# Attention's output and gathered expert tiles turned by transposing transfers, in a fused attention, feed-forward and expert kernel

## The chip, the cores and the metric

The program runs on one core of a Trainium2 chip. The metric is the device time of one execution in microseconds: before the change 768.54 us, the median of 3 runs (767.34 to 770.0). The profiled execution is a run of its own: 772.55 us, of which 770.8 us lie between its first and its last instruction (the span).

## The reference

```
B, H, S, D = 4, 8, 768, 48
# attention: a decayed running state, one 48x48 matrix for each of 32 heads
for t in range(S):
    state = alpha[:, :, t, :, None] * state + einsum('bhd,bhe->bhde', k[:, :, t], v[:, :, t])
    y[:, :, t] = einsum('bhd,bhde->bhe', q[:, :, t], state)
x = y.transpose(0, 2, 1, 3).reshape(3072, 384)
# first feed-forward: w_in 384x2048, w_out 2048x384
h = x @ w_in
x = maximum(0.01 * h, h) @ w_out
# eight experts, each token goes to the one with the largest logit; w1 384x1024, w2 1024x384
logits = x @ w_gate
e = argmax(logits); gate = softmax(logits)[e]
out[token] = gate * (maximum(x[token] @ w1[e], 0) @ w2[e])
```

All inputs and the output are float32. The kernel holds most matrix operands as pairs of float16, a high and a low part, and multiplies high by high, high by low and low by high. So each product of the feed-forward and of the experts is three matmuls.

## The kernel before

**Units.** The 3072 tokens are cut into 8 units of 384. For a unit, attention works on three chunks of 128 tokens, and then the first feed-forward takes the unit as a whole. For one chunk, `chunk` makes scores on TensorE (L710), masks them on VectorE (L715, L717), multiplies them with the values (L741 in units 2 to 7, L747 in units 0 and 1) and adds what the state gives (L754). This leaves the 128x384 result `yp` in PSUM with tokens on the partitions. VectorE takes the largest absolute value (L763), ScalarE writes the scaled result as float32 to `xh` (L767), TensorE turns it in three 128x128 pieces (L777; L775 in units 0 and 1), and ScalarE and VectorE write the high and low parts of the turned result to `xT` (L781, L789). The feed-forward's first product, "hidden" below, reads `xT` (L825, 144 matmuls a unit), its second product reads the activated `gh` (L834, 144 matmuls a unit).

**Routing.** After a unit's second product `route` picks each token's expert and scatters its row (float16 high and low part, gate, token number) with three indirect transfers on GpSimd's queue (L967) to a table `x2_rows` in HBM, ordered by expert. `gather` fetches 128 rows of one expert into a tile `acc` with an indirect transfer (L1198), for which `place_of` copies the tile's row numbers on VectorE (L1195). `turn` turns a gathered tile on TensorE with six float16 transposes (L1212) and copies the result on ScalarE to `XT` (L1214).

**Experts.** There are 26 tiles. 14 of them (`NA`) are full with the rows of units 0 to 6 alone and are gathered before the last unit's scatters; 12 are gathered after these, and 4 of these 12 are split between two experts. The experts' inner width of 1024 is worked off in 4 phases of 256, and each phase passes over all 26 tiles: 104 steps of 18 matmuls (L1334, "hidden") and 6 wider ones (L1363). A step also copies a slice of W1 chosen by a register (`stage`, L1251, VectorE), takes the relu in two parts (L1342 on ScalarE, L1346 on VectorE), and adds into `acc` (L1374 to L1381). For split tiles a second slice comes by a transfer from SBUF to SBUF (`so`, L1261). While one phase runs, the next phase's weights are loaded in 16 pieces of 384 KB on SyncE's queue (L1093) through three buffers and split into high and low parts (in phase 0 on ScalarE L1129 and VectorE L1505, later also on GpSimd).

**What sets the order.** Every engine works off its instructions in the order in which they are written. Up to the end of the feed-forward that order comes from a planner, `Loom`: each piece of work is a generator that yields operations `O` with an engine letter (P TensorE, V VectorE, A ScalarE, G GpSimd, D SyncE's transfers), an assumed duration, and rings of buffers that it takes and frees; the planner keeps a clock for each engine. From the first expert step on the order is written out in `experts`, one pass of its loop for each step; `AHEAD1` says how many steps after a tile's gather its turn is written.

## Time and profile before

| | |
|---|---|
| median of 3 runs | 768.54 us |
| profiled execution: time, span | 772.55 us, 770.8 us |
| TensorE busy | 745.1 us, 97% of the span |
| VectorE, ScalarE, GpSimd busy | 607.2, 483.0, 378.7 us |
| transfers | 102.67 MB, 133 GB/s on the mean |
| granted TensorE clock, mean | 0.995 of full |

In a row of the profile stand the start and the duration of an instruction or a group, the engine, the line of the kernel, output and input by name, and in brackets how long the engine sat idle before it and what released it. Matmuls overlap one another, so the times from start to start tell what one costs TensorE, and not the durations. Transfers show the instruction that issues them; when their bytes have landed is seen at whoever waits for them.

### The profile page before, as it was taken

The numbers are of one execution on the slowest core, as the hardware profiler recorded it, in microseconds if no ns is written. First come the engines' busy times: TensorE is split into PE (matmuls) and PEld (weight loads), VectorE is DVE, ScalarE is ACT, GpSimd is POOL, SyncE is SP. The second block draws the span as 40 slices with busy tenths as digits, with TensorE's granted clock in tenths as the row PEclk, the third lists the DMA queues.
The fourth block names the chain that finished last, engine by engine and source line by source line (L and its number), as shares of the span: only waits on it lengthen the run. The fifth ranks groups of instructions, "written<-read, shape, count | busy, mean of one in ns | idle before, by whom it ended". The sixth has DMA issues, their size and how long they took to land.

```text
span 770.8 us, 21013 instructions
## 1 busy us (share of the span) xinstructions
PE 745.1 (97%) x7927; PEld 509.1 (66%) x7927; DVE 607.2 (79%) x1435; ACT 483.0 (63%) x1083; POOL 378.7 (49%) x406
## 2 busy tenths in 40 slices
PE   9999999998999999999999999899999999999994
PEld 4656675665666666656766665557777777777773
DVE  8999986599799879759855547756878899888673
ACT  4877576789866856845864645824676566667530
POOL 9135024451742763571581270553442588786543
PEclk9999999999999999999999999999999999999998
DMA  9914331153436234223001225224287555653341
GB/s 365 372 55 123 125 125 59 61 168 124 158 100 222 73 102 167 84 83 123 3 21 32 63 70 162 78 83 130 93 280 244 169 170 164 192 185 122 130 178 69
DMA packets 53131, 102.67 MB, mean 133 GB/s; under 512 B 4893, under 2 KB 37715, under 8 KB 53024
## 3 DMA queue, kind: packets, MB, share of 16 engines
q1 hardware_dynamic: 39360, 74.03, 29.9%
q0 software_dynamic: 4960, 14.62, 5.5%
q10 hardware_dynamic: 8704, 12.58, 4.8%
q8 instruction: 67, 1.10, 0.6%
q14 instruction: 40, 0.33, 0.1%
HBM read 79.17 MB, written 9.86 MB: 115 GB/s over the span
## 4 chain that ended last, share of the span: by engine, by line
PE 80%; DVE 11%; DMA 3%; issue 2%; ACT 2%; POOL 1%; ACTq 0%; DVEq 0%; POOLq 0%
PE m L834 22%; PE m L825 21%; PE a L1334 12%; PE m L1363 11%; PE a L710 3%; PE m L390 2%; PE a L754 2%; DMA wr<-in_moe_w 2%; PE a L669 1%; PE a L741 1%; PE a L637 1%; DVE st L1251 1%; DVE w L417 1%; DVE w L419 1%; PE a L486 1%
## 5 line engine op out<-in xcount | busy, mean ns | idle before, releaser
L834 PE MATMUL m<-woh,gh 128*128 128x392 f16 x1152 | 201.8, 329 | 0.0
L825 PE MATMUL m<-xT,wih 128*128 128x384 f16 x1152 | 193.8, 326 | 2.5 <-DVE gf L804 2.5
L809 POOL TENSOR_TENSOR gh<-gf,gh 128x384 f16<-128x384 f32 x128 | 119.0, 940 | 132.6 <-ACT gh L807 129.1
L825 PEld LDWEIGHTS <-wih 128*128 128x128 f16 x1152 | 111.8, 98 | 76.0 <-issue 4.7
L834 PEld LDWEIGHTS <-gh 128*128 128x128 f16 x1152 | 110.3, 98 | 73.4 <-issue 1.4
L1363 PE MATMUL m<-W,hs 128*128 (+1 forms) x624 | 119.1, 326 | 3.2 <-issue 1.8
L1334 PE MATMUL a<-XT,st 128*128 128x128 f16 (+1 forms) x1872 | 117.3, 215 | 3.0 <-DVE st L1251 1.6
L1334 PEld LDWEIGHTS <-st 128*128 128x128 f16 x1872 | 105.9, 98 | 21.0 <-issue 4.7
L804 DVE SCALAR_TENSOR_TENSOR gf<-m,gf 128x384 f32<-128x384 f32 x128 | 70.1, 554 | 55.6 <-ACT gf L802 55.4
L1251 DVE COPY st<-W 128x1536 f16 x104 | 82.7, 795 | 27.4 <-PE a L1334 16.2
L802 ACT ACTIVATE gf<-m 128x384 f32<-128x384 f32 x128 | 62.3, 489 | 42.9 <-PE m L825 39.1
L1342 ACT ACTIVATE hs<-a 128x256 f16<-128x256 f32 x104 | 39.7, 383 | 73.6 <-PE a L1334 52.8
L1363 PEld LDWEIGHTS <-hs 128*128 128x128 f16 (+1 forms) x720 | 57.6, 101 | 32.4 <-issue 3.0
L807 ACT CAST gh<-gf 128x384 f16<-128x384 f32 x128 | 64.4, 507 | 7.4 <-DVE gf L804 7.2
L1133 POOL TENSOR_TENSOR W<-wr,W 128x768 f16<-128x768 f32 x32 | 57.2, 1790 | 7.7 <-ACT W L1132 7.7
L1198 POOL DMA_INDIRECT acc<-x_rows,offj x26 | 30.3, 1164 | 37.3 <-DVE offj L1195 28.4
L1346 DVE SCALAR_TENSOR_TENSOR hs<-a,hs 128x256 f16<-128x256 f32 x104 | 43.2, 415 | 6.1 <-ACT hs L1342 5.4
L1106 POOL TENSOR_SCALAR wr<-wr 128x768 f32<-128x768 f32 x32 | 30.5, 952 | 27.7 <-DMA wr<-in_moe_w 14.9
L351 ACT ACTIVATE scrap<-W 128x768 bf16<-128x768 f16 x48 | 40.2, 838 | 5.9 <-ACT hs L1342 5.5
L1384 POOL DMA_INDIRECT out<-acc x26 | 26.5, 1019 | 31.7 <-DVE acc L1381 20.9
L967 POOL DMA_INDIRECT x_rows<-xg,pi x24 | 25.7, 1071 | 24.7 <-issue 6.4
L728 POOL TENSOR_TENSOR sh<-sm,sh 128x512 f16<-128x512 f32 x17 | 23.4, 1387 | 27.1 <-ACT sh L723 27.1
(279 smaller groups left out, 1238.6 us busy)
## 6 DMA issues: line engine op xcount, KB each, us to landing
wr<-in_moe_w SPq DMA_DIRECT2D x64, 384.0 KB
so<-W ACTq DMA_DIRECT2D x32, 384.0 KB
al<-in_aT SPq DMA_DIRECT2D x16, 390.0 KB
raw_in<-in_moe_w_in SPq DMA_DIRECT2D x12, 512.0 KB
kn__125<-in_kT SPq DMA_DIRECT2D x8, 768.0 KB
qn__126<-in_qT SPq DMA_DIRECT2D x8, 768.0 KB
raw<-in_moe_w_out SPq DMA_DIRECT2D x16, 384.0 KB
ck<-in_moe_w_in SPq DMA_DIRECT2D x24, 256.0 KB
```

The source lines that it names most:

```text
L351: A.activation(scrap, src, AF.Square, scale=scale, accum_out=g_sq[:, i : i + 1])
L802: A.activation(gf, ph[:, 0:UT], AF.Copy, scale=0.01 * CG)
L804: V.scalar_tensor_tensor(gf, ph[:, 0:UT], CG, gf, ALU.mult, ALU.max)
L807: A.copy(gh[:, 0], gf)
L809: E_[e].tensor_tensor(out=gh[:, 1], in0=gf, in1=gh[:, 0], op=ALU.subtract)
L825: T.matmul(ph[:, 0:UT], wih[:, a, kk, f * P : (f + 1) * P], xT[:, b, kk, :], start=(n == 0), stop=(n == 8),)
L834: T.matmul(po[:, 0:ROW], g[f][:, a, c * P : (c + 1) * P], woh_[0][:, b, f, :], start=(n == 0), stop=(n == 3 * NF - 1),)
L1133: G.tensor_tensor(out=lo, in0=raw, in1=hi, op=ALU.subtract)
L1251: V.tensor_copy(out=sth[i % 2].rearrange("p a k f -> p a (k f)"), in_=Wp[ph][0][:, :, ds(reg(V, j), 1), :, :].rearrange("p a e k f -> p a ...
L1334: T.matmul(hp[:, f * P + z * w : f * P + (z + 1) * w], st[z][:, a, kk, f * P : (f + 1) * P], XT[j][:, b, kk, z * w : (z + 1) * w], start=( ...
L1346: V.scalar_tensor_tensor(hs[:, 1].rearrange("p i t -> p (i t)"), hp[:, 0 : 2 * P], 0.0, hs[:, 0].rearrange("p i t -> p (i t)"), ALU.max, A ...
L1363: T.matmul(yp[z * w : (z + 1) * w, 0:DM], hs[:, a, i, z * w : (z + 1) * w], w2, start=(n == 0), stop=(n == 5), skip_group_check=True,)
```

## The change

Three things are changed. First, in units 2 to 7 `chunk` writes the high and low float16 parts of the scaled result side by side, tokens on the partitions, into `x16` (ScalarE and VectorE), and one transposing transfer of 128x768 float16 values on SyncE's queue writes both into `xT`. TensorE's turn and the two copies out of PSUM go. Second, `turn` is one transposing transfer of the same size from `acc` to `XT`, again on SyncE's queue. Third, the last unit's scatters are declared independent of the gathers of the 14 full tiles, the remaining gathers are written in the pattern two, one, two, one to a step, and the planner's numbers for transfers change with it.

```diff
-AHEAD1 = 4
+AHEAD1 = 3
...
-            self.rings[name].drop(key, t)
+            self.rings[name].drop(key, t + (4.0 if last == "D" else 0.0))
...
+        if half:
+            yield O("A", 0.62)
+            x16 = pa.tile([P, DM], F32, tag="xh", name="xh", bufs=2).bitcast(F16)
+            A.activation(x16[:, 0:DM], yp[:, 0:DM], AF.Copy, scale=s1)
+            yield O("V", 0.62, free=[YA, ("n1", (u, c))])
+            V.scalar_tensor_tensor(
+                x16[:, DM : 2 * DM], yp[:, 0:DM], s1, x16[:, 0:DM], ALU.mult, ALU.subtract
+            )
+            yield O("D", 0.8, take=[("xT", u)], free=[("xh", (u, c))], post=[("xT", u, c)])
+            if r["xT"] is None:
+                r["xT"] = pm.tile([P, 2, 3, UT], F16, tag="xT", name="xT", bufs=2)
+            nc.sync.dma_start_transpose(out=r["xT"][:, :, :, sl].rearrange("p a k t -> p (a k) t"), in_=x16)
+            return
...
-            if u < US:
-                T.matmul(o, t, ident, start=(kk == 0), stop=False, skip_group_check=True)
-            else:
-                T.transpose(o, t, ident)
+            T.matmul(o, t, ident, start=(kk == 0), stop=False, skip_group_check=True)
...
-            yield O("V", 0.58, free=[XA], post=[("xT", u, c)])
-            V.tensor_tensor(out=xT[:, 1, :, sl], in0=pxv, in1=xT[:, 0, :, sl], op=ALU.subtract)
...
-        yield O("v", 1.65, post=[("cu", u)], lag=1.0)
+        yield O("v", 1.65, post=[("cu", u)], lag=2.5 if u < NU - 2 else 1.0)
...
+            if last:
+                tc.declare_no_dep(sc.ins, group="full", reason="full tiles hold no row of the last unit")
...
-            if n + RING < NP:
-                start(n + RING)
-            if not fine:
+            if fine:
+                if n + RING < NP:
+                    start(n + RING)
+            else:
                 yield 1.4
+                if n + RING < NP:
+                    start(n + RING)
...
+        if j < NA:
+            tc.add_to_no_dep_group("full", ga.ins)
...
-        px = pst("a").bitcast(F16)
-        x16 = acc[j][:, 0:DM].bitcast(F16)
-        for kk in range(6):
-            T.transpose(px[:, kk * P : (kk + 1) * P], x16[:, kk * P : (kk + 1) * P], ident16)
+        nc.sync.dma_start_transpose(
+            out=XT[j].rearrange("p a k t -> p (a k) t"), in_=acc[j][:, 0:DM].bitcast(F16)
+        )
         state["turned"] = n + 1
-        return lambda: A.copy(XT[j].rearrange("p a k t -> p (a k t)"), px[:, 0 : 2 * DM])
...
-            yield O("PA", (0.4, 0.75), need=[("acc", j)], take=[("a", ("t", j))], free=[("a", ("t", j))])
-            turn(j)()
+            yield O("D", 1.25, need=[("acc", j)])
+            turn(j)
...
-        for j in order[0][NA:]:
+        for n, j in enumerate(order[0][NA:]):
             place_of(j)
             gather(j)
             state["gathered"].append(state["tile"])
-            yield
+            if n % 3:
+                yield
...
-            if t < len(state["gathered"]) and state["gathered"][t] <= i - AHEAD1:
-                turned = turn(t)
+            while state["turned"] < len(state["gathered"]) and state["gathered"][state["turned"]] <= i - AHEAD1:
+                turn(state["turned"])
...
-            next(firsts, None)
+            for _ in range(2):
+                next(firsts, None)
```

TensorE around the start of unit 2's hidden product, before: `diag`, `qt`, `kt`, `vt` are attention's operands, `xh` is the result to be turned, `xT` the turned result.

```order
L754 MATMUL a<-diag_111,qt 64x96 x8
L637 MATMUL a<-ident,kt 128x128 x4
L834 LDWEIGHTS gh
L834 MATMUL m<-woh,gh 128x392
...
L637 MATMUL a<-ident,kt 128x128 x4
L669 MATMUL a<-vt,kn 64x48 x8
L777 MATMUL a<-ident,xh 128x128 x3
L710 MATMUL a<-qt,kt 64x128 x16
L825 LDWEIGHTS wih
L825 MATMUL m<-xT,wih 128x384
```

The same place after (lines of the changed kernel: L752 is L754 before, L840 is L834, L635 is L637, L708 is L710, L831 is L825):

```order
L752 MATMUL a<-diag_110,qt 64x96 x8
L840 LDWEIGHTS gh
L840 MATMUL m<-woh,gh 128x392
...
L635 MATMUL a<-ident,kt 128x128 x8
L708 MATMUL a<-qt,kt 64x128 x16
L831 LDWEIGHTS wih
L831 MATMUL m<-xT,wih 128x384
```

The turn of the last chunk has left TensorE's order, and so has the state's matmul L669, which now stands behind the first 27 hidden matmuls.

GpSimd between the last gathers of full tiles and the first ones after them, before, with the buffers' numbers: `acc12`, `acc13` are the last two full tiles, `xg` holds one chunk's rows of the last unit.

```order
L1198 DMA acc12_6333<-x2_rows,offj_68 128x386
L966 COPY xg_7346<-con_100 128x1
L967 DMA x2_rows<-xg_7346,pi_7893 32769x386
L966 COPY xg_7474<-con_100 128x1
L967 DMA x2_rows<-xg_7474,pi_7893 32769x386
L966 COPY xg_7601<-con_100 128x1
L967 DMA x2_rows<-xg_7601,pi_7893 32769x386
L1198 DMA acc13_6334<-x2_rows,offj_68 128x386
L1198 DMA acc22_7973<-x2_rows,offj_68 128x386
```

The same place after (L1209 is L1198 before, L973 is L967):

```order
L1209 DMA acc12_6445<-x2_rows,offj_67 128x386
L1209 DMA acc13_6446<-x2_rows,offj_67 128x386
L972 COPY xg_7272<-con_99 128x1
L973 DMA x2_rows<-xg_7272,pi_7790 32769x386
L972 COPY xg_7384<-con_99 128x1
L973 DMA x2_rows<-xg_7384,pi_7790 32769x386
L972 COPY xg_7468<-con_99 128x1
L973 DMA x2_rows<-xg_7468,pi_7790 32769x386
L1209 DMA acc22_7851<-x2_rows,offj_67 128x386
```

The gather of tile 13 has moved from behind the last unit's three scatters to ahead of them.

SyncE in the middle of expert phase 0, before: `wr` is a piece of the next phase's weights.

```order
L1093 DMA wr_8267<-in_moe2_w1 128x3x256
L1093 DMA wr_8270<-in_moe2_w1 128x3x256
L1093 DMA wr_8325<-in_moe2_w1 128x3x256
L1093 DMA wr_8381<-in_moe2_w2 128x2x384
L1093 DMA wr_8455<-in_moe2_w2 128x2x384
```

The same place after (L1101 is L1093 before, L1224 is the transposing transfer of `turn`):

```order
L1101 DMA wr_8161<-in_moe2_w1 128x3x256
L1224 DMA_TRANSPOSE XT22_7489<-acc22_7851 128x6x128
L1224 DMA_TRANSPOSE XT14_7481<-acc14_7493 128x6x128
L1101 DMA wr_8219<-in_moe2_w2 128x2x384
L1224 DMA_TRANSPOSE XT15_7482<-acc15_7494 128x6x128
L1224 DMA_TRANSPOSE XT23_7490<-acc23_7852 128x6x128
L1224 DMA_TRANSPOSE XT16_7483<-acc16_7495 128x6x128
L1101 DMA wr_8363<-in_moe2_w2 128x2x384
L1224 DMA_TRANSPOSE XT17_7484<-acc17_7496 128x6x128
```

The last 12 tiles' transposing transfers now stand between the weights' transfers, and each waits on this queue for its gather.

## Rows read from the trace of the kernel before

**Rows 1.** Page: busy us, share and instructions of each engine; the chain by engine.
```profile
PE 745.1 (97%) x7927; PEld 509.1 (66%) x7927; DVE 607.2 (79%) x1435; ACT 483.0 (63%) x1083; POOL 378.7 (49%) x406
PE 80%; DVE 11%; DMA 3%; issue 2%; ACT 2%; POOL 1%; ACTq 0%; DVEq 0%; POOLq 0%
```

**Rows 2.** Stretches: us, busy PE, PEld, DVE, ACT, POOL, clock, DMA share, GB/s.
```profile
150.00:200.00 50.00, 46.83 (x561) 31.45 (x559) 46.33 (x117) 44.26 (x115) 19.08 (x17) 1.00 0.48 155
200.00:455.00 255.00, 255.00 (x2477) 166.62 (x2476) 194.31 (x491) 164.82 (x373) 127.11 (x135) 1.00 0.28 90
```

**Rows 3.** Groups by line: count, busy us, mean ns, idle before and releaser.
```profile
L1212 PE MATMUL a<-ident,acc 128*128 128x128 f16 x156 | 13.0, 219 | 1.6 <-DMA acc<-x_rows,offj 1.6
L777 PE MATMUL a<-ident,xh 128*128 128x128 f32 x54 | 8.9, 277 | 0.4 <-ACT xh L767 0.4
```

**Rows 4.** TensorE in order of time: start, us, line, idle before and releaser.
```profile
176.54 0.55 PE L777 MATMUL a<-ident,xh 128*128 128x128 f32 x3
176.92 1.66 PE L834 MATMUL m<-woh,gh 128*128 128x392 f16 x9
...
526.26 0.50 PE L1212 MATMUL a<-ident,acc 128*128 128x128 f16 x6
526.60 1.66 PE L834 MATMUL m<-woh,gh 128*128 128x392 f16 x9
```

**Rows 5.** TensorE at the start of unit 2's hidden product.
```profile
179.11 0.88 PE L754 MATMUL a<-diag,qt 128*64 128x96 f32 x16
...
186.44 0.82 PE L825 MATMUL m<-xT,wih 128*128 128x384 f16 x4
```

**Rows 6.** TensorE at the start of unit 7's hidden product.
```profile
484.63 3.08 PE L825 MATMUL m<-xT,wih 128*128 128x384 f16 x18 [1.65 <-DVE gf L804]
```

**Rows 7.** TensorE's expert steps: 0 and 1, 14, 26, then two of phase 2.
```profile
530.75 2.17 PE L1334 MATMUL a<-XT,st 128*128 128x128 f16 x36
...
564.56 0.42 PE L1334 MATMUL a<-XT,st 128*128 128x64 f16 x9
...
596.82 1.18 PE L1334 MATMUL a<-XT,st 128*128 128x128 f16 x18
...
652.52 1.17 PE L1334 MATMUL a<-XT,st 128*128 128x128 f16 x18
654.50 1.17 PE L1334 MATMUL a<-XT,st 128*128 128x128 f16 x18
```

**Rows 8.** VectorE's groups from 564.5 to 596.8 us, steps 14 to 25.
```profile
L1505 DVE SCALAR_TENSOR_TENSOR W<-wr,W 128x768 f16<-128x768 f32 x11 | 10.9, 988 | 0.0
L1251 DVE COPY st<-W 128x1536 f16 x12 | 7.0, 579 | 4.2 <-PE a L1334 2.7 <-PE a L1212 1.3
L1376 DVE TENSOR_SCALAR acc<-m,acc 128x384 f32<-128x384 f32 x10 | 6.1, 614 | 1.3 <-issue 0.8 <-PE m L1363 0.5
L1346 DVE SCALAR_TENSOR_TENSOR hs<-a,hs 128x256 f16<-128x256 f32 x12 | 5.0, 418 | 0.9 <-ACT hs L1342 0.7
L1195 DVE COPY offj<-off 128x1 int32<-128x1 int32 x7 | 1.0, 142 | 0.0
```

**Rows 9.** Last scatters and gathers in order of time, then the turn behind them.
```profile
546.64 1.05 POOL L967 DMA_INDIRECT x_rows<-xg,pi  x1 [3.76 <-DVE hs L1346]
...
549.90 1.01 POOL L967 DMA_INDIRECT x_rows<-xg,pi  x1 [0.28 <-POOL xg L966]
554.70 1.15 POOL L1198 DMA_INDIRECT acc<-x_rows,offj  x1 [3.79 <-DMA x_rows<-xg,pi]
...
558.26 0.51 PE L1212 MATMUL a<-ident,acc 128*128 128x128 f16 x6 [1.62 <-DMA acc<-x_rows,offj]
```

**Rows 10.** Stretches of expert phase 0, columns as in rows 2.
```profile
550.75:596.80 46.05, 42.14 (x596) 33.19 (x594) 35.21 (x79) 31.29 (x53) 17.26 (x15) 1.00 0.74 235
564.50:581.00 16.50, 15.31 (x229) 11.94 (x227) 12.31 (x28) 11.39 (x20) 7.61 (x6) 1.00 0.93 298
```

**Rows 11.** The chain of waits: one stretch of a weights transfer.
```profile
467.91 5.82 DMA wr<-in_moe_w
```

More of the change, by code (lines that the diff above doesn't have):

```diff
@@ L247, in tile_kernel @@
     ident = cp.tile([P, P], F32, name="ident")
-    ident16 = cp.tile([P, P], F16, name="ident16")
     ej = cp.tile([P, NT], I32, name="ej")
@@ L315, in tile_kernel @@
     make_identity(nc, ident)
-    G.tensor_copy(out=ident16, in_=ident)
     trif = tm.tile([P, P], F32, name="trif")
@@ L764, in chunk @@
         s1, r["e1", c] = pow2(mx, K1, 1, "n1")
+        if "xT" not in r:
+            r["xT"] = None
+        if half:
[11 more added lines that the diff above has]
+            return
         yield O("A", 0.62, free=[YA, ("n1", (u, c))])
@@ L767, in chunk @@
         A.activation(xh, yp[:, 0:DM], AF.Copy, scale=s1)
-        yield O("P", 0.35 if u >= US else 0.68, take=[XA, ("xT", u)], free=[("xh", (u, c))])
-        if "xT" not in r:
+        yield O("P", 0.68, take=[XA, ("xT", u)], free=[("xh", (u, c))])
+        if r["xT"] is None:
             r["xT"] = pm.tile([P, 2, 3, UT], F16, tag="xT", name="xT", bufs=2)
@@ L781, in chunk @@
         A.copy(xT[:, 0, :, sl], pxv)
-        if u < US:
-            yield O("P", 0.2)
-            T.matmul(pxv, idn16, xT[:, 0, :, sl], start=False, stop=True, skip_group_check=True)
-            yield O("A", 0.52, free=[XA], post=[("xT", u, c)])
-            A.copy(xT[:, 1, :, sl], pxv)
-        else:
-            yield O("V", 0.58, free=[XA], post=[("xT", u, c)])
-            V.tensor_tensor(out=xT[:, 1, :, sl], in0=pxv, in1=xT[:, 0, :, sl], op=ALU.subtract)
+        yield O("P", 0.2)
+        T.matmul(pxv, idn16, xT[:, 0, :, sl], start=False, stop=True, skip_group_check=True)
+        yield O("A", 0.52, free=[XA], post=[("xT", u, c)])
+        A.copy(xT[:, 1, :, sl], pxv)
     def scores_range(u, c, s_):
@@ L1197, in gather @@
     def gather(j):
-        G.indirect_dma_start(
+        ga = G.indirect_dma_start(
             out=acc[j].bitcast(I32),
@@ L1310, in tile_kernel @@
     loom.run()
-    state["gathered"] = [int((t - loom.clock["P"]) / 2.3) for t in state["gathered"]]
+    state["gathered"] = [int((t - loom.clock["P"]) / 2.0) for t in state["gathered"]]
     pm_ctx.close()
@@ L1485, in experts @@
                 while state["turned"] < min(i + 1, NM):
-                    turn(state["turned"])()
+                    turn(state["turned"])
                 hp = hidden(i)
-            t, turned = state["turned"], None
-            if t < len(state["gathered"]) and state["gathered"][t] <= i - AHEAD1:
-                turned = turn(t)
+            while state["turned"] < len(state["gathered"]) and state["gathered"][state["turned"]] <= i - AHEAD1:
+                turn(state["turned"])
             if i >= 3:
                 accumulate(i - 3, yps.pop(i - 3))
-            next(firsts, None)
+            for _ in range(2):
+                next(firsts, None)
             if i < n - 2:
@@ L1508, in experts @@
             if i < n:
-                if turned:
-                    turned()
                 if i + 4 < n:
```

## The prediction

> **What bounds the kernel now.** The page comes first. TensorE is busy for 745.1 of 770.8 us and the chain of waits runs through it for 80% of the span, VectorE following with 11% [rows 1]. An engine that full gives back what is taken from it, but only where it is itself what ends last, so the second view is busy time by stretch. From 200 to 455 us TensorE is busy in all 255 us, VectorE in 194. From 150 to 200, where unit 2's attention runs, TensorE idles for 3.2 us and VectorE is busy in 46.3 of 50 [rows 2]. The third view is the pitch of the expert steps, start to start. In phase 2 a step takes 654.50 - 652.52 = 1.98 us, TensorE's own work. Phase 0, from its first step at 530.75 to step 26 at 596.82, takes 66.07 us for 26 steps, where 26 x 1.98 is 51.5 [rows 7]. So most of what can be won or lost outside the removed matmuls lies there. Its second half, steps 14 to 25, takes 596.82 - 564.56 = 32.3 us, and VectorE's five groups fill 10.9 + 7.0 + 6.1 + 5.0 + 1.0 = 30.0 of them [rows 8]. There VectorE is the bound, not TensorE. The transfers are the fourth view: they keep the 16 DMA engines busy for 0.74 of the time from 550.75 to the end of phase 0, and for 0.93 at 298 GB/s in its middle [rows 10].
>
> **The change, part by part.** The sum is made against the profiled execution's 772.55 us, of which 1.75 lie outside the span. It ran 0.5% slower than the median of the runs shown, so the result is multiplied by 768.54 / 772.55 = 0.9948.
>
> *Attention's turns in units 3 to 7.* The change takes away 54 matmuls, 3 in each of 18 chunks, whose busy time is 8.9 us [rows 3]. That counts overlap twice. From the first of three to the next product's start it is 176.92 - 176.54 = 0.38 us a chunk [rows 4]. In units 3 to 7 there are 15 chunks in a stretch that TensorE fills: 15 x 0.38 = 5.7 us. ScalarE loses one copy a chunk and VectorE trades one operation for another on the same 384 columns. The new transfer is hidden there: in the changed order at least 63 long matmuls (some 10 us at 1.66 us for 9) [rows 4] stand between the last chunk's result and the hidden product that reads it. The cover would go if it took longer than that.
>
> *Unit 2.* Here the cover is thin. Before, 186.44 - 179.11 = 7.3 us pass from the start of the last chunk's state product to the first hidden matmul [rows 5]. After, only three L840, eight L635 and sixteen L708 stand between, about 3 us of work, and the new path is: the state product 0.9 us, VectorE's maximum and small operations 1 us, ScalarE 0.6, VectorE 0.6, issue, transfer and landing of the transfer. For the last I use the only landing the trace shows for 128 rows of this size: a gather that ended its issue at 555.85 was waited for until 558.26, 2.4 us [rows 9], and add 1.4 for issue and movement. That gives 6.9 us against 7.3, without queueing on VectorE. It can gain the 0.7 us that a shorter queue gives or lose 3 if the operations queue. I take 0.
>
> *Five turns in the feed-forward's tail.* A turn costs TensorE 526.60 - 526.26 = 0.34 us [rows 4]; five stand ahead of phase 0: 1.7 us.
>
> *Start of unit 7's product.* TensorE waits 1.65 us there for VectorE, which is held by phase 0's weights and their transfers [rows 6]. After, attention's end and with it these weights stand earlier in the order. The gain is between 0 and 1.8; I take the middle, 0.9.
>
> *Expert phase 0.* T0 is its first step. Three limits hold it. TensorE with no turns: 14 steps of 1.98 and about 1 us for its start and the last routing make 28.7 us up to step 14. VectorE from there: 30.0 less the 1.0 of row-number copies, which move to steps 9 to 16, is 29.0. So it cannot end ahead of T0 + 57.7, a gain of 8.4. The last unit's scatters, which waited 3.76 us behind gathers, come that much earlier. Their bytes are ready for the next gather 3.79 us after the last one, at 554.70 before [rows 9], at T0 + 20.2 after. Then 1.15 us of issue and 2.4 to land, and 1.4 + 2.4 for the transposing transfer, make T0 + 27.6. Step 14 is due at T0 + 28.7, so it does not wait, and the wait of 1.62 us on tile 13 [rows 9] goes too. The third limit is the DMA engines. From 550.75 on they hold 0.74 x 46.05 = 34.1 us of full work [rows 10]. Three pieces of weights, 3 x 393 KB at 298 GB/s = 4.0 us, move ahead of that stretch, and 12 transposing transfers of 197 KB come in at x us each: 30.1 + 12x. The trace has no transposing transfer. The lower end of x is the rate of the busiest stretch, 197 KB / 298 GB/s = 0.66 us [rows 10]. The upper end is a bad transfer: the chain stands 5.82 us on the weights' queue for 393 KB [rows 11], half of that is 2.9 us. I take 1.0, near the first row, since that stretch also holds copies from SBUF to SBUF, and half as much again because two-byte values are rearranged. Then 42.1 us of work end phase 0 at T0 + 62.1: a gain of 4.0.
>
> The Trainium skill (DMA: Bandwidth & Descriptors, Issuing engines are not separate DMA queues) says that transfers from all issuing engines run on the same 16 DMA engines and interleave. The trace agrees: the share reaches 0.93 when three queues have work. By that rule ring time adds up, and it makes the second rival below. The same page of the Trainium skill (Latency and other measured facts) gives transposing transfers 261 GB/s; an estimate from it is x = 0.75 us, and the sum would be 753. The Trainium skill elsewhere (Advanced Engine Details and Errata, DGE: Hardware vs Software) rates hardware-generated transposes as the worse kind, without a figure. No run here shows either yet.
>
> The sum: 5.7 + 0 + 1.7 + 0.9 + 4.0 = 12.3 us. 772.55 - 12.3 = 760.25, times 0.9948 is 756.3 us. Phases 1 to 3 and the tail keep their work.
>
> **The rivals.**
>
> *The DMA engines eat phase 0's gain.* With x = 1.33 the work is 46.1 us and phase 0 ends where it did. For it: 0.93 of the time is taken already, and tiles and weights share one queue in order, so a piece of weights behind a tile waits for that tile's gather. Against it: 0.74 over the whole stretch leaves room. Gain 8.3, time 760.3.
>
> *Attention comes late.* Loads of later units stand on SyncE's queue behind transfers that wait for VectorE, so attention, and not TensorE, could set units 3 to 7, and the 5.7 us would stay idle. For it: VectorE is at 194 of 255 us there and near its limit in unit 2 [rows 2]. Against it: the DMA share is 0.28 and the order gives each unit's chunks a long lead. Gain 6.6, time 762.0.
>
> *Slower: the transposing transfers pace the last 12 tiles.* One mechanism: in phase 0 each tile's transfer occupies the DMA engines, or its queue, for longer than a step, and TensorE waits at each tile from 14 on. It decides from the point where 30.1 + 12x passes 46.05 + 8.3, the gain of the other parts: x = 2.0 us. At x = 2.9 phase 0 grows by 18.8 us, the total by 10.5: 783.05, or 779.0 on the median's scale. For it: nothing in the trace bounds a transposing transfer but copies. Against it: it would have to run at a third of the rate of the busiest stretch. A false dependency that serialised the transfers would look the same; the change would then not do what it says.
>
> **How the numbers follow.** My forecast has a chance of 0.55, with its own range of 750 (all gains at their ends: 5.7 + 0.7 + 1.7 + 1.8 + 8.4 = 18.3 us) to 760. DMA filling up has 0.15, late attention 0.15, slow transfers 0.15. A change of 0.3%, 2.3 us, is about what a measurement of this kernel can tell from none. Faster by more holds all of the first case, 0.14 of the second and 0.11 of the third: 0.80. Within 0.3%: 0.01 + 0.04 + 0.01 = 0.06. Slower: 0.14 of the last. The range of 749 to 769 leaves out nearly all of the slow case and a few hundredths at the fast end.
>
> **What would show it.** Right: 54 and 156 matmuls gone; the stretch from 200 to 455 us still without idle time on TensorE, and shorter by 5 to 6; no wait of L831 on a transfer beyond 3 us in unit 2; the scatters with no wait of 3.8 us; phase 0 at about 62 us with VectorE's groups back to back; DMA share near 0.9 from T0 + 20. Wrong: TensorE waiting at steps 14 to 25 for `XT`, VectorE waiting for `wr` behind tiles on SyncE's queue, gaps on TensorE ahead of units 3 to 7, or phase 0 longer than 66 us.

## The result, and the profile after

The changed kernel takes 779.41 us (median of 4 runs, 776.52 to 780.03) against 768.33 us (4 runs): a ratio of 1.0135, with a 95% interval of 1.0103 to 1.0166. It is slower. The forecast was 756.3 us, with a range up to 769.0.

The span grew from 770.8 to 778.0 us. Two milestones cut the 7.2 us. The experts' first step T0 comes at 530.28, 0.47 earlier. Phase 0 lasts from 530.28 to 608.25, 77.97 us where it was 66.07 [rows 7]: 11.9 longer. From step 26 to the end it takes 169.75 us, 4.2 less than in the profiled execution of before; the same stretch took 168.6 to 174.0 us in f1 to f3, g2 and g4 below, which all turn the expert tiles as the kernel before does. So the 174.0 us (770.8 - 596.8) of the execution profiled before lie at the upper end of what this stretch takes without the change, and the 4.2 are not put down to it. The first two make 11.4 us; the medians differ by 11.1.

TensorE at the start of unit 2 (start, us, line; idle before and releaser), which answers to [rows 5]:

```profile
182.92 1.97 PE L635 MATMUL a<-ident,kt 128*128 128x128 f32 x8 [3.71 <-POOL kt L610]
186.37 1.98 PE L708 MATMUL a<-qt,kt 48*64 48x128 f32 x32 [1.48 <-DVE qt L612]
188.29 3.06 PE L831 MATMUL m<-xT,wih 128*128 128x384 f16 x9
```

Two waits, neither on a transfer of the change, and then nine hidden matmuls in 3.06 us. The granted clock is at its lower level there, 0.50 of full, 1.2 of 2.4 GHz, from 183 to 191 us. Before, the first nine took 1.64 us at the full clock:

```profile
186.44 1.64 PE L825 MATMUL m<-xT,wih 128*128 128x384 f16 x9
```

By stretches, for [rows 2], [rows 10] and the stretch before the last scatters land (columns as there; the third row is of the kernel before):

```profile
150.00:200.00 50.00, 44.81 (x518) 29.98 (x517) 42.85 (x113) 40.71 (x107) 18.57 (x18) 0.90 0.53 165
200.00:455.00 255.00, 253.97 (x2462) 163.19 (x2461) 191.43 (x494) 159.50 (x360) 128.84 (x138) 1.00 0.35 101
518.00:550.00 32.00, 31.00 (x339) 23.62 (x338) 21.01 (x92) 15.24 (x28) 13.69 (x17) 1.00 0.41 119
518.00:550.00 32.00, 27.96 (x246) 19.49 (x244) 20.23 (x82) 6.31 (x15) 15.55 (x17) 0.95 1.08 210
550.75:596.80 46.05, 33.33 (x402) 25.24 (x400) 27.54 (x73) 15.89 (x30) 14.49 (x13) 0.85 0.97 222
```

The DMA engines, whose share from 518 to 550 us was 0.41 in the kernel before, are full from 518 us on. (The share sums the times of the packets that start in a stretch, so it can pass 1.) The clock mean of 0.85 in the last row is TensorE at half clock behind a wait. That wait, among the expert steps (2, 14 and 15; answers to [rows 7]):

```profile
534.29 1.18 PE L1347 MATMUL a<-XT,st 128*128 128x128 f16 x18 [1.84 <-DVE st L1264]
...
571.92 0.64 PE L1347 MATMUL a<-XT,st 128*128 128x64 f16 x9 [7.65 <-DMA XT<-acc]
...
576.87 2.08 PE L1347 MATMUL a<-XT,st 128*128 128x128 f16 x18 [0.95 <-DMA XT<-acc]
```

Step 14 is the first tile behind the last scatters. From 571.92 to 580.66 steps 14 and 15 run at half clock (2.08 us for 18 matmuls, 1.18 at full). The 11.9 us of phase 0 divide so: 0.4 up to step 13, which starts at 562.13 (562.17 before), 7.4 from there to step 14, 2.9 in steps 14 and 15, and 1.2 in the rest. GpSimd and SyncE on the way to that tile, for [rows 9]:

```profile
546.90 1.38 POOL L973 DMA_INDIRECT x_rows<-xg,pi  x1 [1.81 <-DVE xg L970]
...
557.21 1.43 POOL L1209 DMA_INDIRECT acc<-x_rows,offj  x1 [5.91 <-DVE offj L1206]
```
```profile
533.00 18.45 SPq L1224 DMA_TRANSPOSE XT<-acc  x10
559.54 3.78 SPq L1101 DMA_DIRECT2D wr<-in_moe_w  x2
563.42 4.97 SPq L1224 DMA_TRANSPOSE XT<-acc  x2
```

The scatters no longer wait for gathers, but for VectorE, and start at T0 + 16.6 (before: T0 + 15.9). The gather then waits for VectorE's copy of row numbers. Its 64 packets have moved by 561.4 us (the view from 557.2 to 561.4 us stands below). Its tile's transfer stands behind two pieces of weights, one of which waits for VectorE too; it is issued at 563.42, some 2 us after the gather's packets, and TensorE can start 8.5 us after that. What a transfer costs, from the table of issues (count, median us from issue to landing), the queue's share while one transfer had the chip to itself (371 to 376 us; packets, MB, share), and the gather's packets:

```profile
acc<-x_rows,offj POOLq DMA_INDIRECT x26, 6.1
XT<-acc SPq DMA_TRANSPOSE x26, 6.1
xT<-xh SPq DMA_TRANSPOSE x18, 2.8
```
```profile
q1 hardware_dynamic: 800, 0.20, 20.9%
```
```profile
q0 software_dynamic: 64, 0.20, 22.4%
```

So 0.209 x 5 = 1.05 us of all 16 engines for one, and 6.1 us from issue to landing among the expert tiles.

### The profile page after: what moved, and what is told of

It reads as the page before. It is cut to its first block, busy times and chain, and to the rows that moved or that the text cites. A ratio compares the mean times of both kernels' runs of the same rounds, so it can differ in the third digit from the quotient of the medians.

```text
span 778.0 us, 20642 instructions
## 1 busy us (share of the span) xinstructions
PE 737.9 (95%) x7717; PEld 499.8 (64%) x7717; DVE 606.7 (78%) x1434; ACT 457.2 (59%) x1038; POOL 377.2 (48%) x407
## 5 line engine op out<-in xcount | busy, mean ns | idle before, releaser
L840 PE MATMUL m<-woh,gh 128*128 128x392 f16 x1152 | 200.5, 329 | 0.0
L831 PE MATMUL m<-xT,wih 128*128 128x384 f16 x1152 | 194.0, 328 | 2.9 <-DVE gf L810 2.8
L815 POOL TENSOR_TENSOR gh<-gf,gh 128x384 f16<-128x384 f32 x128 | 121.5, 961 | 114.3 <-ACT gh L813 113.3
L831 PEld LDWEIGHTS <-wih 128*128 128x128 f16 x1152 | 112.0, 98 | 78.2 <-issue 6.0
L840 PEld LDWEIGHTS <-gh 128*128 128x128 f16 x1152 | 110.1, 98 | 75.1 <-issue 1.9
L1347 PE MATMUL a<-XT,st 128*128 128x128 f16 (+1 forms) x1872 | 118.7, 217 | 11.9 <-DMA XT<-acc 8.6
L1347 PEld LDWEIGHTS <-st 128*128 128x128 f16 x1872 | 108.0, 99 | 29.6 <-issue 11.7
L1376 PE MATMUL m<-W,hs 128*128 (+1 forms) x624 | 122.0, 332 | 3.7 <-issue 1.3
L1264 DVE COPY st<-W 128x1536 f16 x104 | 84.4, 812 | 30.6 <-PE a L1347 26.3
L1209 POOL DMA_INDIRECT acc<-x_rows,offj x26 | 28.6, 1098 | 38.8 <-DVE offj L1206 31.4
L1397 POOL DMA_INDIRECT out<-acc x26 | 27.6, 1062 | 26.5 <-DVE acc L1394 21.1
L973 POOL DMA_INDIRECT x_rows<-xg,pi x24 | 24.7, 1029 | 29.2 <-issue 7.4
```

Of the source, the lines that this page charges most:

```text
L815: E_[e].tensor_tensor(out=gh[:, 1], in0=gf, in1=gh[:, 0], op=ALU.subtract)
L831: T.matmul(ph[:, 0:UT], wih[:, a, kk, f * P : (f + 1) * P], xT[:, b, kk, :], start=(n == 0), stop=(n == 8),)
L840: T.matmul(po[:, 0:ROW], g[f][:, a, c * P : (c + 1) * P], woh_[0][:, b, f, :], start=(n == 0), stop=(n == 3 * NF - 1),)
L1264: V.tensor_copy(out=sth[i % 2].rearrange("p a k f -> p a (k f)"), in_=Wp[ph][0][:, :, ds(reg(V, j), 1), :, :].rearrange("p a e k f -> p a ...
L1347: T.matmul(hp[:, f * P + z * w : f * P + (z + 1) * w], st[z][:, a, kk, f * P : (f + 1) * P], XT[j][:, b, kk, z * w : (z + 1) * w], start=( ...
L1376: T.matmul(yp[z * w : (z + 1) * w, 0:DM], hs[:, a, i, z * w : (z + 1) * w], w2, start=(n == 0), stop=(n == 5), skip_group_check=True,)
```

## The experiments

All in one table: ratio to before with its interval (none where there is one run), T0, step 14, step 26, length of phase 0, and TensorE's wait for turned tiles. The runs were made in sessions on different chips, with medians of before from 766.6 to 773.3 us; ratios are within a session. The times T0, step 14 and step 26 are those of one profiled execution each.

| run | ratio | T0 | step 14 | step 26 | phase 0 | wait for tiles |
|---|---|---|---|---|---|---|
| before | 1 | 530.75 | 564.56 | 596.82 | 66.1 | 1.6 (gather) |
| changed | 1.0135 (1.0103-1.0166) | 530.28 | 571.92 | 608.25 | 78.0 | 8.6 |
| e1 | 1.0113 (1.0060-1.0165) | 532.74 | 573.09 | 605.85 | 73.1 | - |
| e2 | 1.0249 (1.0185-1.0312) | 535.09 | 577.14 | 616.26 | 81.2 | 4.0 |
| e3 | 1.0109 (1.0059-1.0158) | 529.44 | 568.18 | 602.08 | 72.6 | 6.5 |
| e4 | 1.0298 (1.0252-1.0344) | 534.03 | 578.16 | 621.88 | 87.9 | 7.9 |
| f1 | 1.0019 (0.9990-1.0049) | 529.44 | 563.75 | 597.09 | 67.7 | - |
| f2 | 1.0024 (0.9993-1.0056) | 529.64 | 564.53 | 599.96 | 70.3 | 1.7 (gather) |
| f3 | one run, 770.79 us | 533.91 | 567.90 | 599.29 | 65.4 | 1.8 (gather) |
| f4 | 1.0153 (1.0095-1.0211) | 530.16 | 568.96 | 609.07 | 78.9 | 9.9 |
| g1 | 1.0381 (1.0331-1.0431) | 530.95 | 575.20 | 626.31 | 95.4 | 31.9 |
| g2 | 0.9951 (0.9922-0.9980) | 524.74 | 558.07 | 594.03 | 69.3 | 1.8 (gather) |
| g3 | one run, 787.51 us | 535.67 | 578.54 | 611.01 | 75.3 | - |
| g4 | 0.9991 (0.9966-1.0017) | 531.78 | 563.52 | 597.48 | 65.7 | - |
| h1 | 1.0217 (1.0186-1.0249) | 531.69 | 573.61 | 612.31 | 80.6 | 13.5 |
| h2 | 1.0211 (1.0169-1.0253) | 530.77 | 571.60 | 612.06 | 81.3 | 4.4 |
| h3 | 1.0364 (1.0332-1.0396) | 529.15 | 571.00 | 621.27 | 92.1 | 23.6 |
| h4 | 1.0191 (1.0141-1.0241) | 529.50 | 565.46 | 604.49 | 75.0 | 6.9 |
| i1 | 1.0397 (1.0353-1.0440) | 530.92 | 577.22 | 627.83 | 96.9 | 30.6 |
| i2 | 1.0129 (1.0089-1.0168) | 526.96 | 561.47 | 606.42 | 79.5 | 1.5 |

### Undoing one part of the change

**e1.** `turn` on TensorE again for all tiles, four steps after the gather.

```diff
-        nc.sync.dma_start_transpose(out=XT[j].rearrange("p a k t -> p (a k) t"), in_=...)
+            for kk in range(6):
+                T.transpose(px[:, kk * P : (kk + 1) * P], x16[:, kk * P : (kk + 1) * P], ident16)
+            return lambda: A.copy(XT[j].rearrange("p a k t -> p (a k) t"), px[:, 0 : 2 * DM])
```

> The changed kernel with all 26 expert tiles turned by TensorE again; attention's transposing transfers in units 2 to 7, the independent scatters and the paired gathers stay. Theory R (the expert tiles' transposing transfers keep the 16 DMA engines full from 518 us on, and phase 0 waits for them): phase 0 falls from 78.0 us to 62 to 67, and the whole to 763 to 770 us. Rival Q (not the transfers' size but the place of the scatters and gathers, or late routing, holds phase 0): phase 0 stays above 72 us and the whole above 773.

Rival Q's numbers: phase 0 falls only to 73.1, and the whole, 780.93 us, not at all. The loss is from step 2 to step 5, before a late tile is due: 536.42 to 549.70, 13.3 us, where before took 7.8. There TensorE idles between single matmuls with nothing that the profile names, and then runs at half clock:

```profile
542.72 0.22 PE L1231 MATMUL a<-ident,acc 128*128 128x128 f16 x1 [1.19 <-issue]
544.13 1.61 PE L1382 MATMUL m<-W,hs 128*128 x6 [1.20 <-issue]
```

**e2.** Attention's `if half:` branch off, TensorE's turn as before; expert tiles by transfers.

```diff
-        if half:
+        if u >= 8:
```

> The changed kernel with attention's output turned by TensorE again in units 2 to 7; the 26 expert tiles are still turned by transposing transfers. Theory R: phase 0 stays at 74 to 80 us, TensorE waits 5 us or more for the first tile behind the last scatters, the whole is 773 to 781 us. If attention's transfers were the cause (unit 2's late start and the half clock behind it), the whole falls to 768 or below.

Beyond both: 790.38 us, 1.0249. Unit 2's second product was late here too (225.92; before 212.35) without a transposing transfer in attention.

**e3.** Plain copies in `turn`:

```diff
-        nc.sync.dma_start_transpose(out=XT[j].rearrange("p a k t -> p (a k) t"), in_=...)
+        nc.sync.dma_start(out=XT[j].rearrange("p a k t -> p (a k t)"), in_=...)
```

> The changed kernel, but the 26 expert tiles' transposing transfers are plain copies of the same 197 KB from the same buffer to the same buffer, in the same place on SyncE's queue and with the same waits; the tiles are not turned, so the experts multiply rows that are not transposed. Theory R: the rearranging is what fills the DMA engines; with it gone the engines' share in phase 0 falls from above 1.0 to about 0.75, the long wait on the first late tile falls from 7.65 us to under 2, phase 0 to 60 to 66 us, the whole to 762 to 769. Rival Q (the order on SyncE's queue, the added bytes and the waits for the gathers): the wait stays at 6 us or more and the whole above 774.

The wait at step 14 stays at 6.5 us and the whole at 780.70: rival Q's side, though the engines' share fell (0.75 from 550.75 to 596.80, where it was 0.97). Phase 0 is 5.3 us shorter than in the changed kernel, of which the times show nothing clear of noise.

**e4.** `turn` on TensorE for the full tiles only.

```diff
+        if n < NA:
+            ...                         # as in e1
         nc.sync.dma_start_transpose(...)
```

> The changed kernel with the 14 full tiles turned by TensorE again; the 12 late tiles still by transposing transfers. Theory R: the ten transfers issued from 533 to 551 us no longer fill the engines while the last scatters land, so these land in about 3.8 us instead of 5.9, the wait at the first late tile falls to 3 to 5 us, phase 0 is 66 to 72 us, the whole 767 to 774. If only the late twelve matter, phase 0 stays above 75 us.

Theory R is refuted: this is the slowest so far, with a phase 0 of 87.9 us, though the engines' share from 518 to 550 us fell from 1.08 to 0.46. As in e1, TensorE stands between single matmuls in steps 3 and 4 (1.20 us, twice), so the run does not tell what the late twelve cost alone.

### The order edits

**f1** is before with the third edit's expert part (independent scatters, two gathers a step). **f3** is before with `lag=2.5`. **f2** is before with attention's transfers, **g4** the same with `lag=2.5`, **g2** the same as f2 from unit 3 on (`if u >= 3:`). **f4** is the changed kernel with one gather a step and `lag=1.0`.

```diff
# g2, against f2
-        if half:
+        if u >= 3:
# f4, against the changed kernel
-        yield O("v", 1.65, post=[("cu", u)], lag=2.5 if u < NU - 2 else 1.0)
+        yield O("v", 1.65, post=[("cu", u)], lag=1.0)
-            for _ in range(2):
-                next(firsts, None)
+            next(firsts, None)
```

> The kernel before with the third edit's part in the expert phase alone: scatters independent, gathers two to a step; no transposing transfer, and every other engine's order as before. New theory S (the order edits hold much of the loss: two gathers to a step put three more copies of row numbers and register loads on VectorE into steps 1 to 3, which carry the last routing, and TensorE, left waiting, drops to half clock): steps 2 to 5 get later by 2 to 6 us, phase 0 takes 68 to 73 us, the whole is 2 to 7 us slower than before. Theory R (only transposing transfers cost): equal to before, or up to 4 us faster since the scatters no longer wait for gathers.

Measured 1.0019: no loss that can be told, and no gain. The scatters start 1.3 us earlier against T0, but the first late gather only at T0 + 24.9 (before 24.0): it waits 6.18 us for VectorE's copy of row numbers.

> The kernel before with one number of the planner changed, the time after which routing's step counts as done (2.5 for 1.0 us in units 0 to 5), which moves some 1,000 rows of TensorE's order and no amount of work. Theory S: TensorE waits 2 to 4 us more around unit 2's start, runs there at half clock for some us, unit 2's second product starts 5 us late or more, the experts' first step is 3 to 5 us later than 530.75 us. Otherwise: the experts' first step within 1 us of before, and unit 2's loss belongs to the transfers.

In its one execution T0 is 3.2 us later: the number alone costs that. Taking it back does not save unit 2 once attention's transfers are in:

> The kernel before with attention's transposing transfers in units 2 to 7 alone: expert tiles turned by TensorE, gathers one to a step, scatters as before, the planner's number for routing as before (1.0 us where the changed kernel has 2.5). Theory S: unit 2's first product starts within 1 us of before, the 5 to 7 us of removed matmuls arrive at the experts' first step (524 to 527 us), phase 0 stays at 66 us, the whole is 4 to 7 us faster than before. If attention's transfers themselves cost what unit 2 lost: the experts' first step stays at 530 us or later and the whole equals before or is slower.

T0 gains 1.1 of the 4 to 7 expected. In f2 and g4 TensorE's wait at unit 2 reads:

```profile
186.25 0.59 PE L949 MATMUL a<-oh,con 128*128 128x24 f32 x2 [5.04 <-DVE rex L943]
```
```profile
183.59 1.93 PE L637 MATMUL a<-ident,kt 128*128 128x128 f32 x8 [3.70 <-POOL kt L612]
```

With 1.0 the planner puts a matmul of routing ahead of data that VectorE delivers 5 us later; with 2.5 it is attention's keys instead.

> The kernel before with attention's transposing transfers in units 2 to 7 and the planner's number for routing at 2.5, as in the changed kernel; turns of expert tiles, gathers and scatters as before. It differs from the first experiment (ratio 1.011) by the gathers one to a step and the scatters in their old place. If the pairs are what made that one slow: phase 0 66 to 70 us, the whole within 0.4% of before. If the planner's number with attention's transfers did it: the whole is 0.8% or more slower.

Within noise of before, and so is f2 with the number at 1.0. So e1's 1.1% needs the pairs of gathers as well, and by f1 the pairs alone do not make it. What they need beside them is seen in **g3** (below), which has the pairs and the number 2.5 and turns everything on TensorE; its own added transfers are issued from 718.7 us on. In its one execution TensorE stands in the same steps, without any transfer of the change:

```profile
546.50 0.22 PE L1360 MATMUL a<-XT,st 128*128 128x128 f16 x1 [0.77 <-issue]
547.24 0.22 PE L1360 MATMUL a<-XT,st 128*128 128x128 f16 x1 [0.52 <-issue]
```

Step 6 starts at T0 + 21.8 there, at 15.3 with the pairs alone (f1), at 13.3 with the number alone (f3) and at 13.2 before. So pairs and number together cost some 8 us of phase 0, in profiles of one execution each; the pairs alone cost 2 there, the number alone nothing.

> The kernel before with attention's transposing transfers in units 3 to 7 alone; unit 2 and all expert tiles are turned by TensorE, every engine's order is that of before up to the end of unit 2's second product. Theory R (the 15 chunks' 5.7 us are real, and only unit 2's start lost them): TensorE has no wait around unit 2 that before did not have, the experts' first step comes at 524 to 527 us, the whole is 0.5 to 0.8% faster than before (762 to 764 us). Rival (what is won ahead of the experts is lost to weights and transfers that then come late): the first step is earlier by 4 us or more, but phase 0 grows by as much and the whole stays within 0.3% of before.

Theory R: T0 comes 6.0 us earlier, the waits at unit 2 are those of before, and the whole is 0.5% faster (0.2 to 0.8). Phase 0 takes 3.2 us more and keeps part of it. This version is the only one faster than before.

> The changed kernel with two order edits taken back: full tiles' gathers one to a step, and the planner's number for routing 1.0. All 44 transposing transfers stay. Theory S: the experts' first step at 524 to 528 us, steps 2 to 5 lose 2 to 4 us less, phase 0 takes 68 to 74 us (the transfers still hold up tiles 14 and on), the whole is 764 to 771. Theory R: phase 0 stays above 76 us and the whole above 773.

Theory R's side: steps 2 to 11 run as fast as before, and phase 0 is still 78.9, with 9.9 us of waiting for turned tiles. Four kernels with attention's transfers now make a square: without the order edits and without the tiles' transfers (f2) 1.0024, with the order edits alone (e1) 1.0113, with the tiles' transfers alone (f4, which keeps the independent scatters) 1.0153, with both 1.0135. Either is enough for the loss, and the two do not add.

### The expert tiles' transfers by themselves

**g1** is before with the second edit alone; **h1** writes each transfer one step after its gather (`AHEAD1 = 1`), **h2** issues the last 16 tiles' by `nc.scalar`, **h3** copies as in e3.

```diff
# h1, against g1
-AHEAD1 = 3
+AHEAD1 = 1
# h2, against g1
-        nc.sync.dma_start_transpose(
+        (nc.scalar if n >= NA - 4 else nc.sync).dma_start_transpose(
```

> The kernel before with the 26 expert tiles' transposing transfers alone (turned three steps after the gather where TensorE's turn stood four after); attention turned by TensorE, gathers, scatters and the planner's number as before. Theory R (each of these transfers holds the 16 DMA engines for about 1.3 us and 24 of them fall into phase 0): the experts' first step is 1 to 2 us earlier than before, TensorE waits for turned tiles, phase 0 takes 74 us or more against 66.1, the whole is 1.0 to 2.0% slower than before. Rival I (they cost only together with the other edits): phase 0 stays under 69 us and the whole within 0.4% of before or faster.

29.3 us on phase 0 and 3.8% on the whole, where 2% was the most expected. Waits of TensorE, and of SyncE's queue in phase 0 (total, times, longest):

```profile
PE a L1350 <- DMA XT<-acc: 31.9, 8, 6.9
```
```profile
SPq L1106 <- DVE W L1520: 38.7, 11, 6.4
```

One turn of it, on TensorE, VectorE and SyncE:

```profile
580.01 0.56 DVE L1267 COPY st<-W 128x1536 f16 x1 [1.79 <-PE a L1350]
580.49 0.42 DVE L1362 SCALAR_TENSOR_TENSOR hs<-a,hs 128x256 f16<-128x256 f32 x1
580.82 0.14 DVE L1211 COPY offj<-off 128x1 int32<-128x1 int32 x1
580.88 0.95 DVE L1520 SCALAR_TENSOR_TENSOR W<-wr,W 128x768 f16<-128x768 f32 x1
```
```profile
581.90 0.37 SPq L1106 DMA_DIRECT2D wr<-in_moe_w  x1
582.36 1.22 SPq L1227 DMA_TRANSPOSE XT<-acc  x1
584.15 0.57 SPq L1106 DMA_DIRECT2D wr<-in_moe_w  x1
584.81 3.12 SPq L1227 DMA_TRANSPOSE XT<-acc  x1
```
```profile
589.96 0.64 PE L1350 MATMUL a<-XT,st 128*128 128x64 f16 x9 [6.91 <-DMA XT<-acc]
```

VectorE copies only after TensorE's step; its split then frees a buffer at 581.83; SyncE issues the weights at 581.90 and the tile behind them; TensorE waits for the tile until 589.96, 7.6 us after its issue.

> The kernel with the expert tiles' transposing transfers alone (ratio 1.038), but each transfer is written one step after its gather instead of three; no work added or removed. Theory L (two chained transfers of some 6 us each stand where one transfer and 1 us of TensorE and ScalarE stood, and a step is 2 us long: the lead is too short): the two steps of extra lead take 8 us or more off the 29.4 us that TensorE waits for turned tiles, the whole is 790 us or less against 802.6. Theory E (the transfers' engine time): the waits stay above 24 us and the whole above 795. Theory Q (SyncE's queue): worse, since the weights then stand behind transfers that wait for their gathers.

Theory L: the wait falls by 18 us, the ratio from 1.0381 to 1.0217. SyncE now waits 29.3 us for gathers instead.

> The kernel with the expert tiles' transposing transfers alone, but those of the last 16 tiles are issued by ScalarE instead of SyncE, so no piece of weights stands between them on one queue. Theory Q: the waits for turned tiles fall below 12 us, the whole below 785. Theories L and E: waits stay above 20 us and the whole above 792 (ScalarE's 1.2 us of issue a tile is hidden in its idle half).

Theory Q's numbers, 4.4 us and 784.19. The same transfers on another queue, and TensorE hardly waits for tiles. But part of the waiting has only moved: ScalarE stands until 557.76 for a gather before it can issue a tile's transfer, and is late with the relu:

```profile
560.10 2.08 PE L1379 MATMUL m<-W,hs 128*128 x6 [5.85 <-ACT hs L1358]
```

> The kernel with the expert tiles' transfers alone, made plain copies of the same 197 KB in the same places with the same waits; the tiles are not turned, so the experts multiply rows that are not transposed. Theory E: the waits fall below 10 us and the whole to 780 or less. Theory L: a copy is a second transfer in the chain all the same; TensorE still waits 12 us or more and the whole stays at 785 or above.

Theory L: TensorE still waits 23.6 us, 8.3 less than in g1, and the whole is 795.37 us. 1.0364 against 1.0381: on the whole time the turning adds nothing that can be told. The Trainium skill (Advanced Engine Details and Errata, X-Bar Transpose (TRN2)) says that such transfers run as fast as regular ones, and by the whole time the runs agree.

**h4** is the changed kernel with `AHEAD1 = 1`; **i1** is g1 with each piece of weights issued a step later; **i2** is the changed kernel with unit 2 turned by TensorE, with `lag=1.0` and both of these.

> The changed kernel, each expert tile's transposing transfer written one step after its gather instead of three. Theory L: the 7.65 us wait at the first tile behind the scatters falls to under 5 us and phase 0 to 70 to 75 us, the whole 1 to 1.5 times 0.5% better than the changed kernel. Theories E and Q: no change beyond 0.3%, or slower.

Undecided: in the profile, which is of the fastest of its four runs, the wait at step 14 falls to 3.97 us, step 14 starts at T0 + 36.0 instead of 41.6, and phase 0 falls to 75.0; the times (775.31 to 786.25 us) show nothing of it.

```diff
+            elif ph == 1:               # the weights loaded while phase 0 runs
+                yield 1.4
+                due.append(n + RING)    # started at the top of the next piece
             else:
                 yield 1.4
                 if n + RING < NP:
                     start(n + RING)
```

> The kernel with the expert tiles' transposing transfers alone (ratio 1.038), with one thing moved: while phase 0 runs, each piece of the next phase's weights is issued about one step later, when VectorE has done with its buffer, instead of in the step before. VectorE's, TensorE's and GpSimd's orders stay word for word. Theory Q, as a circle (a turned tile's transfer stands on SyncE's queue behind a piece of weights, this waits for VectorE's split, that stands behind a copy that waits for TensorE, and TensorE waits for the tile): SyncE's 38.7 us of waiting for the split fall below 20, TensorE's 31.9 us of waiting for turned tiles below 18, the whole to 790 or less. If the circle is not the cause: TensorE's waits stay above 26 us and the whole above 796.

TensorE waits 30.6 us and the whole is 800.00, the numbers of the side on which the circle is not the cause. But the edit did not do its part: SyncE still waits 30.4 us for the split, and 18.2 for gathers. So it neither breaks the circle nor refutes it.

> The changed kernel with four things mended: unit 2 turned by TensorE, the planner's number for routing 1.0, tiles' transfers one step after the gather, weights a step later as in the run beside this one. By the runs so far: the experts' first step at 523 to 526 us, TensorE waits 2 to 6 us for turned tiles, phase 0 takes 69 to 75 us, the whole lies between 0.5% faster and 0.5% slower than before, and above the kernel with the transfers of units 3 to 7 alone (0.995).

Missed: 1.0129. TensorE waits 1.5 us for tiles, and yet phase 0 is 79.5: it now waits for the slices of split tiles, at a DMA share of 1.31 from 570 to 580 us.

```profile
PE m L1390 <- DMA so<-W: 12.2, 3, 6.3
```

**g3**, the transfers at the very end, gave no answer to its question: they were issued from 718.7 us on, in the middle of other traffic.

> Both changes of order as in the changed kernel, all turns on TensorE, and at the very end, when nothing else moves, eight transposing transfers of 197 KB one behind the other and then eight plain copies of the same 197 KB between the same kinds of buffers. If a transposing transfer holds the DMA engines for 1.3 us or more, the eight take 10 to 16 us and move about 100 to 160 GB/s at a share near 1, while the eight copies take 4 to 6 us. If it is only slow in contention, the eight take under 8 us.

## Why the prediction was wrong

**"Expert phase 0", the term of 4.0, is the step that failed.** It was 11.9 the other way. Its sum has step 14's tile ready at T0 + 27.6, in time for a step due at T0 + 28.7; the tile came at T0 + 41.6 (571.92 - 530.28), 7.65 us after TensorE was free for it. Four of its sentences failed.

- "The last unit's scatters, which waited 3.76 us behind gathers, come that much earlier." They did not (T0 + 16.6 after, 15.9 before). [rows 9] names VectorE's L1346, and no gather, as what ended that wait. f1 takes the gathers out of it without any transfer and gains nothing, since the next gather's row numbers are written on VectorE in step 10 either way. The first late gather, at T0 + 20.2 in the sum, began at T0 + 26.9.
- "1.15 us of issue and 2.4 to land, and 1.4 + 2.4 for the transposing transfer", 7.35 us. From the gather's issue to TensorE's first matmul it took 571.92 - 557.21 = 14.7. The gather's part held: its packets had moved within 4.2 us of its issue, against 3.55. The transposing transfer, 3.8 in the sum, was issued some 2 us later, behind weights, and took 8.5 us from there. Its 2.4 came from the landing of a gather [rows 9]; in the stretch that the change itself fills, the tiles' transfers took 6.1 us on the median, and attention's, elsewhere, 2.8. TensorE's turn cost 0.34 us and started when the gather landed; its replacement is a second transfer in the chain, written three steps after the gather where the turn stood four after. That the lead is too short is shown with the tiles' transfers alone (h1) and at step 14 of the changed kernel (h4), where the time did not follow; h3 shows that most of the cost is the hop and not the turning.
- "Three pieces of weights move ahead ... 12 transposing transfers come in." The engines' sum began at T0 + 20, and the queue stood only in the rival of the full DMA engines, as "a piece of weights behind a tile". With the tiles' transfers alone the reverse order did harm: tiles behind weights that wait for VectorE. SyncE waited 33 us for VectorE's split in phase 0 before too; nothing urgent was behind it then. Off that queue (h2) the wait for tiles falls from 31.9 to 4.4 us, though TensorE then waits 6.7 us for ScalarE's relu and 4.9 us for VectorE's sums, and a tile that is late behind these does not show. In the changed kernel the queue held the first late tile for some 2 of the 14.7 us. The ten full tiles' transfers from 533 to 551 us were not counted either; what they cost is not shown, since e4 takes them away and gains nothing.
- "14 steps of 1.98 and about 1 us for its start and the last routing make 28.7 us up to step 14." Without the wait for the tile, step 14 would have started at T0 + 34.0. From T0 to step 5 it took 14.5 us, where before took 10.8; the turns and the wait for tile 13 that are gone gave 3.2 of the 3.6 back by step 13. The order edits stand in the sum with no cost at all, and by e1 they are enough, beside attention's transfers, for a loss of about 1%.

The disputed size was about right: x was taken as 1.0 and measured 1.05 alone, and (0.368 x 778.0 - 0.299 x 770.8) / 44 = 1.27 on the mean from the queue's share before and after. With 1.27 the sum gives a gain of 0.7 and still no loss. The Trainium skill (DMA: Bandwidth & Descriptors, Latency and other measured facts) gives 261 GB/s; here 197 KB in 1.05 us are 188, and the measurement decides. The slow rival named the right place and 779.0 us, but from x = 2.9, and it was to decide only from 2.0: its time was right by chance.

**Ahead of T0: 8.3 us forecast, 0.47 came.** The 5.7 us of units 3 to 7 are real (g2: 6.0). Unit 2 was taken as 0 with a loss of up to 3; it lost about 5 (its second product starts at 218.08, before 212.35), from an order of the planner that the transfers force (f2, g4) or its number makes (f3). Some 2.5 of that are longer waits (5.2 us in two, against 2.7), and the rest comes from the half clock behind them, which the bounds left out. Unit 7's wait, 1.65 [rows 6], was to shrink by 0.9 and was 1.97 us.

**The scale.** Multiplying by 0.9948 spread over the whole sum 4 us by which one execution was longer than the median; they may have lain in its last stretch alone, 174.0 us where the same work takes 168.6 to 174.0.

## What to carry over

Taking work off a full engine paid here where the replacement had long cover (g2), and not where it stood in a just-in-time chain (g1): count the lead in steps against the landing time of the loaded stretch, not of a quiet one. Before a transfer is put on a queue, look at what the instruction ahead of it there waits for, even if that wait cost nothing until now. When a wait goes, read what ended just before it: that is the next wait. Changes of order that ride along with a change need a price of their own, and a run with all of them together but without it.

## What the runs showed that was not expected

- A plain copy of 197 KB and a transposing one cost the kernel the same, as far as can be told (h3, g1), though the transposing one moves packets of 250 bytes on the mean (0.20 MB in 800).
- A transposing transfer holds the issuing engine's queue for at least 1.21 us (1.58 on the median among the expert tiles of the changed kernel), a plain one on SyncE for at least 0.37 to 0.47.
- In e1, e2 and e4 TensorE stood still for 1.2 to 1.7 us between matmuls, and in g3 for up to 1.0, with nothing named that it waits for, in the steps when gathers are issued back to back. All four have the pairs and the number 2.5. What holds it stays open.
- The tiles' transfers by themselves cost 29 us of phase 0 (g1), and 13 in f4, beside attention's transfers and the independent scatters. Why they cost less there stays open.
